# Scores of two batches in one set of 64x64 tiles, and routing per pair of batches, in an attention and soft-MoE kernel

## The chip, the cores and the metric

One core of one Trainium2 chip runs the kernel. Its engines are PE (TensorE: matmuls into PSUM), DVE (VectorE), ACT (ScalarE), POOL (GpSimd) and SP (SyncE, which here issues every DMA). The metric is the device time of one launch in microseconds, and lower is better.

## The reference

Attention with pooled keys and values, and behind it a soft mixture of experts over all tokens:

```python
# q, k, v: (8 batches, 8 heads, 576 tokens, 64); phi: (8, 8, 576, 32)
a = softmax(phi, axis=2)                                   # over the 576 tokens
k_m = einsum('bhsm,bhsd->bhmd', a, k); v_m = einsum('bhsm,bhsd->bhmd', a, v)
attn = softmax(q @ k_m^T / 8, axis=-1)                     # over 32 pooled slots
x = (attn @ v_m) as (4608 tokens, 512)
logits = x @ moe_phi                                       # (4608, 32)
d = softmax(logits, axis=0)                                # over all 4608 tokens
slot_input = d.T @ x                                       # (32, 512): 4 slots for each of 8 experts
slot_out[e] = relu(slot_input[e] @ w1[e]) @ w2[e]          # 512 -> 1024 -> 512
out = softmax(logits, axis=1) @ slot_out                   # (4608, 512)
```

All data is fp32. The inputs q, k, v and phi are 33 MB, the weights 33.6 MB, the output 9.4 MB.

## The kernel before

`x` is never formed. Per batch, `pool_phi` and `pool_kv` make the pooled keys and values; the pooled values times `moe_phi` (`mphd`) then turn attention probabilities straight into logits.

The code does not issue its instructions in the order in which it is written. Each step is handed to a planner (`Plan.add`) with an engine, an assumed cost, the tiles it reads and writes, and a priority. `Plan.order` goes through the steps as a list scheduler does: of those that could start first by the assumed costs it takes the one with the smallest priority, and it hands out buffers (`Slots`) as they come free. What results is a fixed order for each engine. Without a priority of its own a step has its number in the code, plus `plan.bias`: 60 less for the pooling (so it comes ahead), 110 more for the routing (behind).

One batch goes like this. `pool_phi` takes the maximum of phi over tokens (L498 on DVE, L506 to L531), subtracts it on POOL (L536), takes the exponential on ACT (L542) and sums over tokens (L549 on POOL, L559 on PE, L566 and L567 on DVE). `pool_kv` multiplies phi with k and v on PE (L586), scales on ACT (L602, L609), turns the pooled keys and values by PE (L620, L621) and multiplies the values with `moe_phi` (L629). `attend` turns q in 32x32 blocks on DVE (`q_blocks`, L665), and then goes through two halves `a` of a batch: `scores` on PE (L698: 16 matmuls on 32x32 tiles of the array into `scbank`), a DVE transpose that reads `scbank` (L712), the softmax (maximum L729 on DVE, subtraction L734 on POOL, exponential L739 on ACT, sum L744 on DVE, L749 on ACT, reciprocal L753 on DVE, product L757 on POOL), a DVE transpose of the probabilities (L762), and `transposed`: PE transposes (L773) with ACT copies (L778), which put tokens on partitions and heads and slots on columns. `logits` multiplies the probabilities with the value products (L793), copies (L805), turns by PE (L811) and copies (L818) into `L`, 96 partitions of tokens.

`route` is the token softmax of one batch: the maximum over its tokens (L831, L838, L843, L849), the difference (L857), the exponential (L866), the routing sums of probabilities (L875, the 96 tokens of a group as contraction), and from them the batch's share of `slot_input` (L897, L901, L908, L925), stored in `SIU` with its maximum in `MB` and its sum in `SD`. The merge (L960 to L991) scales the eight batches to a common maximum and adds them up into `SIM`, on DVE for the most part. Then come the experts on PE (L1055, L1080, L1104), with the token-side softmax (`slots`, L1128 to L1167) beside them, and the output (L1194 to L1226, stores L1234).

Space: most buffers lie in one SBUF tile, `arena`, of 44,288 columns. Attention's buffers are stacked from its start, 30,172 columns; the weights come in 19 slots of 2,048 columns (1 MB) that fill it from its end. So six slots are free from the start, and the others as attention gives up its buffers. The 32 weight loads stand in SP's one queue with the inputs; 13 of them go into a slot for the second time, after an expert has read the first load. Filler matmuls (L463) stand on PE where the planner finds it idle, at the start and at the end of attention.

Of the kernel before, what the change touches and what calls it, by code (L numbers as in the profile page):

```python
# [20 lines left out]
class Plan:  # L21
# [14 lines left out]
    def __init__(self):  # L36
        self.ops = []
        self.last_w = {}
        self.reads = {}
        self.bias = 0  # L40

    def add(self, eng, cost, fn, r=(), w=(), also=(), pri=None, dma=0.0, slack=0.0):
        i = len(self.ops)
        deps = set()
        tiles = set()
        for x in r:
            for key in x:
                tiles.add(key[0])
                if key in self.last_w:
                    deps.add(self.last_w[key])  # L50
        for x in w:
            for key in x:
                tiles.add(key[0])
# [15 lines left out]
        self.ops.append((eng, cost, fn, deps, i + self.bias if pri is None else pri, dma, tiles, need, slack))  # L69
# [177 lines left out]
def kernel(  # L247
# [38 lines left out]
    JG = 3  # L286
    NG = J // JG
    Y = 32
    R = HALF // Y
    T = JG * Y  # L290
    X = R * NG
    U = R * J
    JY = J * Y

# [17 lines left out]
    b_o = Slots(banks, [(i, 1) for i in range(4)], (b_m,))  # L312
# [5 lines left out]
    PHI_SZ, KV_SZ, AT_SZ = C * J * M, 2 * C * J * D, X * (2 * CM + 2)  # L318
    Q_SZ, QT_SZ, KT_SZ, EX_SZ, TR_SZ = C * J * D, C * J * D // 2, 3 * P, 2 * U * M, 2 * U * Y
# [10 lines left out]
    def shaped(off, shape):  # L330
# [4 lines left out]
        if len(shape) == 2:  # L335
            a = a.rearrange("p (a b) -> p a b", a=shape[0])
        elif len(shape) == 3:
            a = a.rearrange("p (a b c) -> p a b c", a=shape[0], b=shape[1])
# [8 lines left out]
    def stack(shape, n, fifo=False):  # L347
# [11 lines left out]
    NSEG = B  # L359
    mphi_b = stack([C, NS], 1).tile()  # L360
    kps = stack([2, P], 2)
    dm1s, wdgs = stack([NS], 2), stack([NS], 2)
    vms = stack([2, D], 4, fifo=True)
    vprs = stack([2, NS], 3, fifo=True)
    lgTs = stack([R, T], 2)
    trees = stack([C, 4, M], 1)
    pmxs, pmbs, pess = stack([C, M], 2), stack([C, M], 2), stack([C, M], 2)
    dfs = stack([X, NS], 2)
    wts = stack([2 * CM + 2], 2)
    wtbs = stack([2, C, NS], 2)  # L370
# [6 lines left out]
    attns = stack([AT_SZ], 2, fifo=True)  # L377
    aTs, sexs = stack([TR_SZ], 2), stack([EX_SZ], 2)
    kTs, qTs = stack([KT_SZ], 2, fifo=True), stack([QT_SZ], 3)
# [12 lines left out]
    repa_b = keep("repa", [P, NS])  # L392
    ones_b = keep("ones", [P, P])
    mphd_b = keep("mphd", [P, C, 2, NS])
    ident, maskhp, maskc, rep, repa, ones, mphd = (
        x.ap for x in (ident_b, maskhp_b, maskc_b, rep_b, repa_b, ones_b, mphd_b)
# [6 lines left out]
    P_AHEAD, R_BEHIND = 60, 110  # L403
# [3 lines left out]
    def f():  # L407
        nc.vector.memset(ones, 1.0)
        for i in range(2):
            a = attns.aps[i].rearrange("p (x y) -> p x y", x=X)  # L410
            nc.vector.memset(a[:, :, 2 * CM:], 1.0)
# [859 lines left out]
```

## Time and profile before

Three runs of the kernel: 229.35, 230.9 (the median) and 231.32 us. The profiled execution has a span of 229.8 us; the page gives no other time of it.

| What | Profiled execution |
|---|---|
| first DVE transpose of scores (L712) | 24.9 us |
| last q turned (L665) | from 120.0 us |
| merge begins (L960) | 146.8 us |
| first expert matmul (L1055) | 155.3 us |
| first matmul with the last weights (L1104) | 195.6 us |
| end | 229.8 us |
| busy: PE, DVE, ACT, POOL | 185.0, 139.3, 86.9, 85.0 us |
| moved by DMA | 76.5 MB, 333 GB/s over the span |

Times count from the first instruction. Engines wait for each other by semaphores; the profile names for each idle stretch of an engine the instruction that ended it. A matmul's own duration overlaps with those of its neighbours, so for PE the busy time of a group is read, not the mean of one. L numbers are lines of the kernel, as in the listing above.

### The profile page before, as it was taken

What the parts mean: (1) busy time and instruction counts of PE and PEld (TensorE: products, weight loads), DVE (VectorE), ACT (ScalarE), POOL (GpSimd) and SP (SyncE); (2) the same over time, 40 slices, a digit from 0 to 9 for tenths busy, and PEclk for the clock granted to TensorE, in tenths of its full rate; (3) what the DMA queues carried; (4) which work ended last, traced back from release to release, by engine and by line L of the source; (5) the groups of instructions that cost most, each with busy time, mean ns of one, the idle gap of its engine ahead of it and who ended that gap; (6) DMA issues with size and microseconds to landing.
All of it is one profiled execution on the core that took longest, in us unless ns stands there. A gap on an engine that the chain in (4) does not pass through costs nothing.

```text
span 229.8 us, 6394 instructions
## 1 busy us (share of the span) xinstructions
PE 185.0 (81%) x2772; PEld 109.7 (48%) x2772; DVE 139.3 (61%) x241; ACT 86.9 (38%) x230; POOL 85.0 (37%) x83
## 2 busy tenths in 40 slices
PE   8998939959978988899887979939999985599400
PEld 6786615626646636644644556624553421164100
DVE  3244696978499887856786681699401960277410
ACT  2022332562654754635546655300102332176300
POOL 2370773998159479266495432030000000000000
PEclk9999995995997997755999988985999999769655
DMA  6999999999999999994592999657999997059994
GB/s 225 383 380 389 379 389 378 393 399 383 347 393 395 387 387 401 345 392 152 185 369 63 418 356 396 240 184 277 347 415 409 409 409 298 0 205 409 414 414 203
DMA packets 27884, 76.50 MB, mean 333 GB/s; under 512 B 1744, under 2 KB 5840, under 8 KB 27856
## 3 DMA queue, kind: packets, MB, share of 16 engines
q1 hardware_dynamic: 27856, 76.09, 87.8%
q8 instruction: 22, 0.36, 0.6%
q14 instruction: 6, 0.05, 0.1%
HBM read 66.65 MB, written 9.44 MB: 331 GB/s over the span
## 4 chain that ended last, share of the span: by engine, by line
PE 44%; DMA 25%; DVE 13%; SPq 4%; ACT 3%; issue 3%; POOL 2%; DVEq 0%; ACTq 0%; POOLq 0%
DMA top<-in_q_dram 13%; DMA arena<-in_moe_w_dram 8%; PE kvbank L586 7%; PE bank L1055 7%; PE scbank L698 5%; PE bank L773 5%; SPq L445 4%; DMA out_dram<-arena 4%; PE bank L1215 3%; PE bank L875 3%; PE bank L793 3%; PE kvbank L1104 2%; PE kvbank L463 2%; DVE arena L665 2%; POOL arena L536 1%
## 5 line engine op out<-in xcount | busy, mean ns | idle before, releaser
L536 POOL TENSOR_TENSOR arena<-arena 128x1152 f32<-128x1152 f32 x8 | 21.0, 2631 | 26.8 <-ACT arena L531 26.8
L463 PE MATMUL kvbank<-ones 128*128 128x256 f32 x90 | 26.9, 441 | 2.1 <-ACT arena L609 1.1
L665 DVE STREAM_TRANSPOSE arena<-top 128x1152 f32<-128x1152 f32 x16 | 21.7, 1360 | 9.1 <-DMA top<-in_q_dram 9.1
L698 PE MATMUL scbank<-arena 32*32 32x288 f32 x512 | 23.1, 471 | 2.8 <-DVE arena L712 2.8
L586 PE MATMUL kvbank<-arena 64*32 64x128 f32 x1152 | 24.0, 315 | 1.2 <-issue 0.9
L549 POOL TENSOR_TENSOR arena<-arena 128x128 f32<-128x128 f32 (+2 forms) x32 | 23.3, 729 | 4.3 <-ACT arena L542 2.4
L757 POOL TENSOR_TENSOR arena<-arena,ssm 128x576 f32<-128x576 f32 x16 | 18.5, 1156 | 16.4 <-DVE ssm L753 16.4
L586 PEld LDWEIGHTS kvbank<-arena 64*32 64x32 f32 x1152 | 19.7, 122 | 7.0 <-issue 3.4
L463 PEld LDWEIGHTS kvbank<-ones 128*128 128x128 f32 x90 | 18.3, 218 | 6.6 <-issue 1.8
L734 POOL TENSOR_TENSOR arena<-arena,smx 128x576 f32<-128x576 f32 x16 | 18.5, 1158 | 7.8 <-DVE smx L729 7.8
L778 ACT COPY arena<-bank 96x384 f32<-96x384 f32 x32 | 14.4, 475 | 17.5 <-PE bank L773 17.3
L712 DVE STREAM_TRANSPOSE arena<-scbank 128x576 f32<-128x576 f32 x16 | 12.3, 768 | 12.5 <-PE scbank L698 12.5
L773 PE MATMUL bank<-ident,arena 128*96 128x128 f32 x96 | 18.1, 339 | 1.5 <-DVE arena L762 1.2
L1055 PE MATMUL bank<-arena,SIM 128*32 128x256 f32 x256 | 16.6, 425 | 3.4 <-DVE SIM L991 3.4
L498 DVE TENSOR_REDUCE arena<-arena 128x128 f32<-128x1152 f32 x8 | 17.4, 2171 | 2.5 <-DMA arena<-in_phi_dram 2.5
L1104 PE MATMUL kvbank<-arena 128*32 128x512 f32 x128 | 15.6, 598 | 3.7 <-DMA arena<-in_moe_w_dram 3.7
L1215 PE MATMUL bank<-sr,cT 128*128 128x512 f32 x36 | 13.5, 508 | 5.0 <-ACT arena L1224 1.9
L773 PEld LDWEIGHTS bank<-ident,arena 128*96 128x96 f32 x96 | 13.2, 157 | 6.3 <-issue 2.7
L1226 DVE COPY arena<-bank 128x512 f32<-128x512 f32 x18 | 11.8, 690 | 6.7 <-DMA out_dram<-arena 3.7
L1055 PEld LDWEIGHTS bank<-arena,SIM 128*32 128x32 f32 x256 | 8.7, 123 | 10.8 <-DVE SIM L991 3.6
L698 PEld LDWEIGHTS scbank<-arena 32*32 32x32 f32 x512 | 8.6, 114 | 10.5 <-issue 4.2
L1224 ACT COPY arena<-bank 128x512 f32<-128x512 f32 x18 | 10.3, 587 | 8.2 <-DMA out_dram<-arena 4.0
(108 smaller groups left out, 264.5 us busy)
## 6 DMA issues: line engine op xcount, KB each, us to landing
arena<-in_moe_w_dram SPq DMA_DIRECT2D x32, 1024.0 KB, 10.6
arena<-in_k_dram SPq DMA_DIRECT2D x8, 1152.0 KB, 10.3
arena<-in_v_dram SPq DMA_DIRECT2D x8, 1152.0 KB, 12.1
top<-in_q_dram SPq DMA_DIRECT2D x8, 1152.0 KB, 14.0
out_dram<-arena SPq DMA_DIRECT2D x12, 768.0 KB, 9.4
arena<-in_phi_dram SPq DMA_DIRECT2D x8, 576.0 KB, 7.7
arena<-in_moe_phi_dram SPq DMA_DIRECT2D x1, 64.0 KB, 9.1
```

What stands on the lines that cost most here:

```text
L463: lambda: nc.tensor.matmul(warm.ap, ones, ones.unsqueeze(1).to_broadcast([P, 2, P]), start=True, stop=True,),
L536: lambda: nc.gpsimd.tensor_tensor(ph(), ph(), mb.ap.unsqueeze(2).to_broadcast([P, C, J, M]), op=ALU.subtract),
L549: plus = lambda o, x, y: nc.gpsimd.tensor_tensor(o, x, y, op=ALU.add)
L586: nc.tensor.matmul(acc.ap[M * c: M * c + M, a, : 2 * D], ph()[h0: h0 + HALF, c, j, :], kv()[h0: h0 + HALF, :, c, j * D: j * D + D], start= ...
L665: nc.vector.transpose(qT.ap.rearrange("p (i u y) -> p u i y", i=2, y=Y), qt.ap[:, h * QT_SZ: h * QT_SZ + QT_SZ].rearrange("p (u i x) -> p ...
L698: nc.tensor.matmul(scb.ap[M * c: M * c + M, r, :JY], kT.ap[h0: h0 + Y, i * P + M * c: i * P + M * c + M], qT[c // 2].ap.rearrange("p (i c ...
L734: lambda: nc.gpsimd.tensor_tensor(exv(), exv(), bc(mx), op=ALU.subtract),
L757: lambda: nc.gpsimd.tensor_tensor(exv(), exv(), bc(sm), op=ALU.mult),
L773: nc.tensor.transpose(tp.ap[:T, t * P: t * P + P], aT.ap[:, x: x + T], ident)
L1055: nc.tensor.matmul(hb.ap[NS * j: NS * j + NS, :256], SIM.ap[:, 2 * i + c, NS * e: NS * e + NS], wv[:, c, 256 * j: 256 * j + 256], start=(e ...
L1104: nc.tensor.matmul(pacc.ap[NS * x: NS * x + NS, 0, :DM], hT()[:, 4 * t + 2 * i + j, NS * e: NS * e + NS], wv[:, j, t, :], start=(e == 0 an ...
L1215: lambda po=po, i=i, ct=cT[bp, j0]: nc.tensor.matmul(po.ap[:, :DM], ct.ap()[:, i * P: i * P + P], sr.ap, start=True, stop=True),
```

## The change

A pair of batches takes the place of one batch. A batch's 576 tokens are 64 rows of 9 (`J`); the rows of two batches fill the 128 partitions.

- **Scores.** A round is now two heads (`c`) of both batches, four rounds per pair in place of two rounds per batch. The pooled keys are written block-diagonally (`kps`, with zeros set once; four PE transposes instead of two, into `kbs`), so that a 64x64 tile of the array takes both 32-row blocks of one head. A round is 8 matmuls, in place of 16 on 32x32 tiles. What DVE's transpose makes of them has tokens on partitions: batch `g`, token of 64; columns head, `J`, slot.
- **Transposes dropped.** Since the softmax already stands with tokens on partitions, `transposed` (L773, L778) goes. The routing sums read the softmax buffer `ex` itself, 288 columns at a time (a block of ones behind it gives the sums), in 18 matmuls per pair with 64 tokens as contraction.
- **Logits.** The value products are written block-diagonally into `vpb` (128x128 for each head). Eight matmuls on the whole array, two for each round, add up a pair's logits in one PSUM bank, which is set aside for them (`b_l`; the other small results have three banks instead of four). One DVE transpose (after's L955) brings them into `L`, 128 partitions of tokens, in place of two ACT copies and two PE transposes per batch.
- **Routing and merge.** `route` runs once per pair, on 128 partitions and 288 columns; the merge is over four segments. `slots` works on 128 partitions with 9 x 32 columns instead of 96 with 12 x 32.
- **Order.** The priorities are given by `plan.at(base, slope)`: pooling of pair `bp` from `bp - 1.15`, loads of q from `bp - 0.45`, score round `c` from `bp + 0.25 c`, routing from `bp + 1.2` (the last one from `bp + 1`). Some assumed costs are set anew, among them that of scores.
- **Loads and space.** The first loads are phi of batches 0 and 1, moe_phi, and then q, k, v of each. Attention's buffers take 34,436 columns of `arena`, so four of the 19 weight slots are free from the start.

The order on SP, at the start of the program. A row is one instruction (x and a count: so many alike in a row): its line, its name, what it writes and reads, the size; `top` holds q, `arena` all else. Before:

```order
L445 DMA arena<-in_phi_dram 128x4x288
L445 DMA arena<-in_k_dram 128x4x576
L445 DMA arena<-in_v_dram 128x4x576
L445 DMA arena<-in_moe_phi_dram 128x4x32
L445 DMA top<-in_q_dram 128x4x576
L445 DMA arena<-in_phi_dram 128x4x288
L445 DMA arena<-in_k_dram 128x4x576
L445 DMA arena<-in_v_dram 128x4x576
L445 DMA top<-in_q_dram 128x4x576
```

And now:

```order
L458 DMA arena<-in_phi_dram 128x4x288 x2
L458 DMA arena<-in_moe_phi_dram 128x4x32
L458 DMA top<-in_q_dram 128x4x576
L458 DMA arena<-in_k_dram 128x4x576
L458 DMA arena<-in_v_dram 128x4x576
L458 DMA top<-in_q_dram 128x4x576
L458 DMA arena<-in_k_dram 128x4x576
L458 DMA arena<-in_v_dram 128x4x576
```

The same nine loads come first; batch 1's v is the last of them now, batch 1's q was.

PE in the middle of attention. `bank` with a number is one of the four small PSUM banks (62 to 65; 65 is the one set aside now), `kvbank` the pooled sums, `scbank` the scores, `pmh` and `dmh` small maxima. Before (a round of scores is the first row, pooling of the next batch stands between):

```order
L698 MATMUL scbank<-arena 32x288 x16
L586 MATMUL kvbank<-arena 32x128 x24
L773 MATMUL bank_64<-ident,arena 96x128 x3
L773 MATMUL bank_62<-ident,arena 96x128 x3
L586 MATMUL kvbank<-arena 32x128 x24
L773 MATMUL bank_63<-ident,arena 96x128 x3
L773 MATMUL bank_65<-ident,arena 96x128 x3
L793 MATMUL bank_64<-arena 32x192 x6
L559 MATMUL bank_62<-maskhp,arena 128x2
L586 MATMUL kvbank<-arena 32x128 x24
L811 MATMUL bank_63<-ident,arena 96x96 x2
L875 MATMUL bank_65<-arena 32x258 x6
```

And now, with L599 for L586, L716 for L698, L785 for the logits and L810 for the maximum in `route`:

```order
L599 MATMUL kvbank<-arena 32x128 x48
L785 MATMUL bank_65<-arena 128x288 x2
L599 MATMUL kvbank<-arena 32x128 x24
L533 MATMUL bank_64<-ident,pmh_83 64x128 x2
L716 MATMUL scbank<-arena 64x288 x8
L572 MATMUL bank_62<-maskhp,arena 128x2
L810 MATMUL bank_63<-ident,arena 32x128
L716 MATMUL scbank<-arena 64x288 x8
L785 MATMUL bank_65<-arena 128x288 x2
L635 MATMUL bank_64<-ident,arena 128x4x32 x4
L640 MATMUL bank_62<-ident,arena 128x128
```

The transposes of probabilities are gone, and two logits matmuls follow each round of scores at some distance.

DVE at the end of attention, up to the first step of the merge. `ssm` and `smx` are sums and maxima of the softmax. Before:

```order
L744 TENSOR_REDUCE ssm_82<-arena 128x18
L762 STREAM_TRANSPOSE arena<-arena 128x576
L753 RECIPROCAL ssm_82<-ssm_82 128x18
L857 TENSOR_TENSOR arena<-L_93,bank_63 96x192
L762 STREAM_TRANSPOSE arena<-arena 128x576
L908 TENSOR_TENSOR arena<-bank_62,maskc 128x256
L831 TENSOR_REDUCE arena<-L_93 96x32
L843 TENSOR_REDUCE dmh_89<-bank_64 32x1
L857 TENSOR_TENSOR arena<-L_93,bank_62 96x192
L960 TENSOR_REDUCE m_95<-arena 128x32
```

And now:

```order
L890 TENSOR_TENSOR arena<-bank_64,maskc 128x512
L761 TENSOR_REDUCE ssm_81<-arena 128x18
L770 RECIPROCAL ssm_80<-ssm_80 128x18
L770 RECIPROCAL ssm_81<-ssm_81 128x18
L777 STREAM_TRANSPOSE arena<-arena 128x576 x2
L955 STREAM_TRANSPOSE L_92<-bank_65 128x288
L803 TENSOR_REDUCE arena<-L_92 128x32
L815 TENSOR_REDUCE dmh_88<-bank_62 32x1
L829 TENSOR_TENSOR arena<-L_92,bank_64 128x288
L969 TENSOR_REDUCE m_94<-arena 128x32
```

The last but one batch's mask product (L908) stood among the last rows; now that of the last but one pair (L890) is ahead of the last softmax sums, and one turn of logits stands where ACT copies fed DVE.

The diff, cut to its core:

```diff
 class Plan:
+    def at(self, base, slope=1.0):
+        self.phase = [base * 1000.0, slope]
...
+        if pri is None:
+            pri = self.phase[0]
+            self.phase[0] += self.phase[1]
...
-    b_m = Slots(banks, [(i, 1) for i in range(4)])
+    b_m = Slots(banks[:3], [(i, 1) for i in range(3)])
+    b_l = Slots(banks[3:], [(3, 1)])
...
-    FIRST = ["phi0", "k0", "v0", "mphi", "q0", "phi1", "k1", "v1", "q1"]
+    FIRST = ["phi0", "phi1", "mphi", "q0", "k0", "v0", "q1", "k1", "v1"]
...
+            for i in range(2):
+                for r in range(R):
+                    nc.tensor.transpose(o[:, i, :, r, :], kp.ap[:, i, r * P: r * P + P], ident)
...
+                    vpp.ap[HALF * g: HALF * g + HALF, HALF * c: HALF * c + HALF],
+                    vT.ap[:, c].rearrange("p r m -> p (r m)"),
+                    mphd[:, c].rearrange("p a n -> p (a n)"),
...
+                    tile_position=(0, HALF * g),
...
+            nc.scalar.copy(
+                vpb.ap[x: x + Y, :, x: x + NS],
+                vpp.ap[x: x + Y, : H * NS].rearrange("p (h n) -> p h n", h=H),
+            )
...
-    def scores(a, qT, kT, ex):
+    def scores(c, qT, kb, ex):
...
+                for a in range(2):
+                    for g in range(2):
+                        h0 = HALF * a
                         nc.tensor.matmul(
+                            scb.ap[HALF * g: HALF * g + HALF, a, :JY],
+                            kb[g].ap[h0: h0 + HALF, i, c].rearrange("p r m -> p (r m)"),
+                            qT[g][c // 2].ap.rearrange("p (i c x) -> p i c x", i=2, c=2)[
+                                h0: h0 + HALF, i, c % 2, :
                             ],
...
+                            tile_position=(h0, HALF * g),
...
-    def transposed(a, r, aT, atb):
-                nc.tensor.transpose(tp.ap[:T, t * P: t * P + P], aT.ap[:, x: x + T], ident)
...
+    def logits(c, aT, vpb, lp):
...
+                h = 2 * c + a
+                nc.tensor.matmul(
+                    lp.ap[:, :JY],
+                    vpb.ap[:, h, :],
+                    aT.ap[:, a * JY: (a + 1) * JY],
+                    start=(h == 0),
+                    stop=(h == H - 1),
                 )
...
-    def route(si, atb, vm):
+    def route(bp, ex, vm):
...
+            for j in range(J):
+                for g in range(2):
+                    x = NS * (j % 4)
                     nc.tensor.matmul(
+                        wp[g].ap[x: x + NS, : HM + M],
+                        dfv()[HALF * g: HALF * g + HALF, j, :],
+                        ev[HALF * g: HALF * g + HALF, :, j, :],
...
+                        tile_position=(HALF * g, x),
...
-    for b in range(B):
-        plan.bias = -P_AHEAD
...
+    for bp in range(NBP):
+        for g in range(2):
+            plan.at(bp - 1.15 + 0.5 * g, 8)
...
+        plan.at(bp - 0.45)
...
+        for c in range(C):
+            plan.at(bp + 0.25 * c, 15)
+            scores(c, qT, kb, ex)
+            aT = softmax(c, ex)
+            logits(c, aT, vpb, lp)
+        add(
+            DVE, dve(JN), lambda lp=lp, bp=bp: nc.vector.transpose(L[bp].ap, lp.ap[:, :JY]),
+            r=[lp], w=[L[bp]],
+        )
+        plan.at(bp + (1.2 if bp < NBP - 1 else 1.0), 10)
+        sip = route(bp, ex, vm)
```

More of the change, by code (lines that the diff above doesn't have):

```diff
@@ L44, in add @@
         deps = set()
-        tiles = set()
+        tiles = {}
         for x in r:
             for key in x:
-                tiles.add(key[0])
+                tiles[key[0]] = None
                 if key in self.last_w:
@@ L52, in add @@
             for key in x:
-                tiles.add(key[0])
+                tiles[key[0]] = None
                 if key in self.last_w:
@@ L391 @@
     rep_b = keep("rep", [P, 4, NS])
-    repa_b = keep("repa", [P, NS])
     ones_b = keep("ones", [P, P])
     mphd_b = keep("mphd", [P, C, 2, NS])
-    ident, maskhp, maskc, rep, repa, ones, mphd = (
-        x.ap for x in (ident_b, maskhp_b, maskc_b, rep_b, repa_b, ones_b, mphd_b)
+    ident, maskhp, maskc, rep, ones, mphd = (
+        x.ap for x in (ident_b, maskhp_b, maskc_b, rep_b, ones_b, mphd_b)
     )
@@ L668, in f @@
                 )
-            add(DVE, dve(QT_SZ), f, r=[qt], w=[qT])
-            halves.append(qT)
-        return halves
-    def attend(b, qt, kT, vp):
-        atb = attns.tile().split(2 * R)
-        Lb = L[b // 2]
-        qT = q_blocks(qt)
-        parts = [(0, 1), (1, 2)]
-        ex, aT = sexs.tile().split(2), aTs.tile().split(2)
-        for a0, a1 in parts:
-            for a in range(a0, a1):
-                scores(a, qT, kT, ex)
-            softmax(a0, a1, ex, aT)
-            for a in range(a0, a1):
-                for r in range(R):
-                    transposed(a, r, aT, atb)
-        logits(b, aT, vp, Lb)
-        return atb
-    def scores(a, qT, kT, ex):
+            halves.append((qT, f))
+        return halves
+    def scores(c, qT, kb, ex):
         scb = b_s2.tile()
@@ L893, in route @@
+        for g in range(2):
+            add(ACT, act(HM) + act(1), lambda f=f, g=g: f(g), r=[wp[g]], w=[wt.part(g)])
         wtp = b_m.tile()
         def f():
-            for a in range(2):
+            for g in range(2):
+                for a in range(2):
+                    x = NS * (2 * g + a)
+                    nc.tensor.matmul(
+                        wtp.ap[:, x: x + NS],
+                        wt.ap[:, g, P * a: P * a + P],
+                        rep[:, 0, :], start=True, stop=True,
+                    )
+            for g in range(2):
@@ L1151, in f @@
                 nc.vector.tensor_tensor(cr[:, :, r, 1, :], cx(), c4[:, :, r, 0, :], op=ALU.subtract)
-        add(DVE, 2.0, f, r=[cxb], w=[csb])
-        for t in range(NG):
+        add(DVE, 1.6, f, r=[cxb], w=[csb])
+        for t in range(J // G):
             tp, ct = b_m.tile(), cTs.tile()
```

430 lines of the change are left out of this document (200 added, 230 removed).

## The prediction

> **What bounds the kernel now.** I read the span first, then the busy time of the engines by stage, then the chain of waits, then the groups of instructions and who waited for whom.
>
> ```profile
> span 229.8 us, 6394 instructions
> 24.90:110.60 85.70, 73.58 (x1527) 45.45 (x1528) 68.47 (x104) 41.77 (x115) 56.62 (x53) 0.80 0.98 362
> 110.60:146.80 36.20, 31.74 (x480) 20.20 (x481) 23.06 (x48) 20.06 (x64) 15.81 (x14) 0.95 0.84 313
> 146.80:155.30 8.50, 4.46 (x32) 2.72 (x31) 7.78 (x13) 1.52 (x5) 2.02 (x1) 0.89 0.44 157
> ...
> 155.34 10.36 PE bank L1055 x144
> ...
> 176.34 19.19 DMA arena<-in_moe_w_dram
> 195.58 1.11 PE kvbank L1104 x8
> ```
>
> The three stage rows give the stretch in us and its length, then the busy us of PE, PE's weight loads, VectorE (DVE), ScalarE and GpSimd, each with its instruction count, then the granted TensorE clock, the DMA share and GB/s. The last three rows are pieces of the chain: start, length, what. Attention runs until 146.8, the merge until 155.3, where the first expert matmul (L1055) starts. From there to the end of the span lie 229.8 - 155.3 = 74.5 us. In them the kernel waits for weights: 13 of the 32 loads of 1 MB can only go into a slot that an expert has emptied, so the last 19 us before L1104 are DMA. That part moves with the start of the experts, one for one; I cost it at nothing, because the change leaves its loads, their number after the merge and their order as they are. So the question is when the first L1055 starts.
>
> In attention no engine is full: from 24.9 to 146.8 (121.9 us) PE is busy 73.58 + 31.74 = 105.3 us (86%), DVE 68.47 + 23.06 = 91.5 us (75%). DVE is idle for 30.4 us. Why, the waits say:
>
> ```profile
> DVE arena L712 <- PE scbank L698: 12.5, 9, 5.1
> DVE arena L665 <- DMA top<-in_q_dram: 9.1, 4, 6.5
> DVE prs L566 <- PE bank L559: 8.6, 5, 2.3
> DVE arena L908 <- PE bank L901: 4.0, 1, 4.0
> ...
> 24.89 0.78 DVE L712 STREAM_TRANSPOSE arena<-scbank 128x576 f32<-128x576 f32 x1 [5.05 <-PE scbank L698]
> ```
>
> The columns of the waits are total us, times and the longest. The first L712 (5.1) and the first L665 (6.5) lie before 24.9. After it DVE waits for PE 12.5 - 5.1 + 8.6 + 4.0 = 20.0 us of its 30.4, and for q 2.6 us. PE and DVE pass the work to and fro, and PE, whose instructions stand in one order, is mostly the later one.
>
> **The change part by part.** First PE, with what is dropped, the rows that price what is new, and the DVE groups:
>
> ```profile
> L773 PE MATMUL bank<-ident,arena 128*96 128x128 f32 x96 | 18.1, 339 | 1.5 <-DVE arena L762 1.2 <-DVE ssm L753 0.3
> L778 ACT COPY arena<-bank 96x384 f32<-96x384 f32 x32 | 14.4, 475 | 17.5 <-PE bank L773 17.3
> L875 PE MATMUL bank<-arena 96*32 96x258 f32 x96 | 10.0, 437 | 0.2 <-ACT arena L866 0.2
> L793 PE MATMUL bank<-arena 128*32 128x192 f32 x96 | 7.5, 356 | 0.0
> L811 PE MATMUL bank<-ident,arena 96*96 96x96 f32 x16 | 3.1, 275 | 0.8 <-issue 0.8
> L629 PE MATMUL bank<-mphd,arena 128*32 128x64 f32 x64 | 2.8, 252 | 0.6 <-ACT arena L624 0.6
> L620 PE MATMUL bank<-ident,arena 128*128 128x128 f32 x16 | 3.4, 297 | 3.0 <-ACT arena L602 2.9 <-ACT arena L918 0.2
> L897 PE MATMUL bank<-repa,arena 96*128 96x32 f32 x32 | 4.8, 273 | 0.0
> L698 PE MATMUL scbank<-arena 32*32 32x288 f32 x512 | 23.1, 471 | 2.8 <-DVE arena L712 2.8
> L831 DVE TENSOR_REDUCE arena<-L 96x32 f32<-96x192 f32 x8 | 3.7, 459 | 1.7 <-ACT L L818 1.7
> L857 DVE TENSOR_TENSOR arena<-L,bank 96x192 f32<-96x192 f32 x8 | 2.7, 338 | 0.7 <-PE bank L849 0.7
> L908 DVE TENSOR_TENSOR arena<-bank,maskc 128x256 f32<-128x256 f32 x8 | 3.3, 417 | 4.2 <-PE bank L901 4.0
> L712 DVE STREAM_TRANSPOSE arena<-scbank 128x576 f32<-128x576 f32 x16 | 12.3, 768 | 12.5 <-PE scbank L698 12.5
> L498 DVE TENSOR_REDUCE arena<-arena 128x128 f32<-128x1152 f32 x8 | 17.4, 2171 | 2.5 <-DMA arena<-in_phi_dram 2.5
> L665 DVE STREAM_TRANSPOSE arena<-top 128x1152 f32<-128x1152 f32 x16 | 21.7, 1360 | 9.1 <-DMA top<-in_q_dram 9.1
> ...
> 136.66 2.08 PE L463 MATMUL kvbank<-ones 128*128 128x256 f32 x4
> ...
> 146.09 1.56 PE L463 MATMUL kvbank<-ones 128*128 128x256 f32 x6
> ```
>
> Busy us stand after the bar, then mean ns of one; since matmuls overlap, I price by busy us per record, and an fp32 matmul leaves two records. Gone from PE: the transposes of probabilities L773 (18.1), the old logits L793 and their turn L811 (7.5 + 3.1), the old token sums L875 (10.0), the old value products L629 (2.8): 41.5 us. New on PE:
>
> - Logits: 8 matmuls per pair of batches on the whole array, 288 columns, so 64 records. A full 128x128 record of 256 columns takes 1.56/6 = 0.26 us where the clock is full (146.09) and 2.08/4 = 0.52 us at its slowest (136.66); times 288/256 that is 0.29 or 0.585 us. I take the fast one, 18.7 us; the slow end is 37.4.
> - Token sums: 144 records. With eight tiles of the array at work instead of three, L875's time scales by records, columns and tiles to 10.0 x (144 x 288 x 3)/(96 x 258 x 8) = 6.3 us; if the tiles don't overlap better than now, 10.0 x 144/96 = 15.0. I take 6.3, since L698 with eight tiles does 512 records in 23.1 us.
> - Value products: 64 records on one tile position, from 2.8 (as now) to 9.6 (64 at L897's 4.8/32 = 0.15): I take 5.
> - Transposes of the pooled keys: 16 more at L620's 3.4/16 = 0.21: 3.4 us.
> - Scores: half as many records on tiles four times as large, four at a time instead of eight: the same array time, so 0.
>
> That is 33.4 us taken (bounds 31 and 65), so PE loses 41.5 - 33.4 = 8 us of 105 (bounds: 10 less, 24 more). ScalarE loses L778's 14.4 us and gains copies; it was busy 61.8 of 121.9 us, so neither counts.
>
> DVE's softmax groups keep their counts and shapes. Four reduces, subtractions and mask products replace eight, on 288, 288 and 512 columns instead of 192, 192 and 256: by size 4 x 0.459 x 1.5 = 2.8 for 3.7, 4 x 0.338 x 1.5 = 2.0 for 2.7, and 4 x 0.417 x 2 = 3.3 for 3.3. Four new transposes of logits at half of L712's 0.768 add 1.5. Sum 0 (bounds 1 each way).
>
> The start. The scores of a pair need the pooled keys of both its batches, so the first ones wait for the second batch's v.
>
> ```profile
> 26.91 2.25 PE L586 MATMUL kvbank<-arena 64*32 64x128 f32 x144
> ...
> 19.48 0.62 ACT L602 ACTIVATE arena<-kvbank,prs 128x128 f32<-128x128 f32 x2 [6.44 <-PE kvbank L463]
> ...
> 26.63 1.38 DVE arena L665
> ```
>
> The first nine loads are the same bytes in both kernels; the last of them, q of batch 1, lands at 26.6 (L665 starts). Now v of batch 1 is last, so the pooling (2.25 us) ends near 29. From ScalarE's pooled keys (19.48) to the first score transpose (24.89) the old kernel took 5.4 us, with filler matmuls between; with a little less of that I put the first score transpose at 33.5, which is 8.6 us later. DVE does not lose all of it: three L498 and four L665 (3 x 2.17 + 4 x 1.36 = 12) stand ahead of it in place of two each (7), and the two row maxima and reciprocals behind them add about 1: 6 us of later work is done by then. Net +2.7 (bounds 0 and 5).
>
> DVE's idle time. Two thirds of it (20.0 of 30.4) is waiting for PE. Where PE is asked for 8 us less, at least 8 x 20.0/30.4 = 5.3 us of that should go; the 4.0 us that DVE waited in the last stretch for L901 are behind other softmax work in the new order, so I take 7 (bounds 0 and 20).
>
> The merge, 8.5 us now, works on four segments instead of eight:
>
> ```profile
> 148.34 1.09 DVE L969 TENSOR_TENSOR arena<-arena 128x896 f32<-128x896 f32 x1 [0.48 <-ACT arena L966]
> 149.46 1.68 DVE L972 TENSOR_REDUCE arena<-arena 128x128 f32<-128x896 f32 x1
> ```
>
> Three stored segments instead of seven: 2.77 x 4/7 = 1.6 us less (bounds 0, if the last token sums come later than DVE, and 2.5).
>
> Loads. Four weight loads instead of six fit before attention gives up its space; two more (2 x 1 MB at 313 GB/s = 6.7 us) must pass between the last inputs and the experts. DMA stood idle 16% of 36.2 and 56% of 8.5 us there, 10.6 us: they fit, and the inputs end earlier by as much. Zero, with 3 as the other end.
>
> Sum: +2.7 - 7 - 1.6 = -5.9 us, all ahead of the first L1055: it starts at 149.4, and the span is 223.9. The three runs have a median of 230.9, 1.1 above the profiled span; the page shows no time around that execution's span, so I add the same 1.1: **225.0 us**.
>
> **The rivals.** A change below 1% (2.3 us) can't be told from none here.
>
> *PE was the whole brake.* If DVE's waiting for PE all goes (20.0), the next limit is the input.
>
> ```profile
> 119.97 1.37 DVE L665 STREAM_TRANSPOSE arena<-top 128x1152 f32<-128x1152 f32 x1
> ```
>
> The inputs and four weight loads, 37.3 MB at the stretch's 362 GB/s, are in at 103; from the last L665 to the experts the old kernel needed 155.3 - 120 = 35 us. So 138, 17 us earlier: 214 us. For it: PE's 86%. Against: the last pair turns its q and runs four softmax rounds after that point, not two.
>
> *No change.* The idle time keeps its length, with waits for PE replaced by those of a larger unit: a pair's logits close only when its fourth round is done, and one PSUM bank holds them. Then +2.7 - 1.6 = +1.1, 232 us. For it: the first scores come 8.6 of a pair's 121.9/4 = 30 us later, and DVE can't be refilled from another pair.
>
> *Slower: the clock.* If gaps in PE's work bring its clock down, the new matmuls cost more than the transposes that they replace.
>
> ```profile
> 44.00:50.00 6.00, 3.47 (x137) 2.40 (x121) 5.43 (x11) 2.47 (x9) 5.77 (x6) 1.00 1.04 406
> 50.00:56.00 6.00, 5.80 (x119) 3.66 (x127) 4.83 (x8) 2.96 (x8) 5.76 (x8) 0.58 1.05 378
> 98.00:104.00 6.00, 6.00 (x69) 2.88 (x75) 3.71 (x4) 2.34 (x7) 3.78 (x2) 0.50 1.05 392
> 110.00:116.00 6.00, 4.99 (x107) 3.31 (x88) 4.08 (x10) 3.56 (x13) 2.99 (x2) 1.00 0.71 255
> ```
>
> After a stretch in which PE was busy 3.47 of 6 us the clock was 0.58. If PE, with less to do, stays there, the logits cost 37.4 us and the sums and products up to 15.0 and 9.6: 24 us more on PE in all, and by the same two thirds 16 us on the path; in full that is +17 (248 us), half way 240. It decides from 2 us more on PE than now (0.66 x 3.5 + 1.1 = 2.3 above zero), that is, from a granted clock between 25 and 110 well under the 0.80 of now. Against it: at 98 to 104 the clock was 0.50 with PE busy all 6 us, and at 110 to 116 it was 1.00 with 4.99, so gaps alone don't set it. The Trainium skill ("TensorE: Matmul & The Clock Gate", Part 1) says that an idle window of about 3.4 us halves the clock and that activity releases it: by that rule less PE work is a risk, and the first two rows agree, the last two don't. The same page (Part 4) says that transposes don't count as activity: by it, dropping 96 of them raises the clock, which speaks against this rival.
>
> That the transposes are not dropped is excluded: they don't stand in the new order.
>
> **How the numbers follow.** Forecast 0.50, its own range 219 to 229. PE the whole brake 0.16 (214). No change 0.18 (229 to 233). The clock 0.16 (236 to 248). Faster by over 1% is the forecast but for its last tenth, and the first rival: 0.62; within 1%: 0.04 + 0.18 = 0.22; slower: 0.16. For 8 in 10 the range runs from 213, just past the first rival, to 236, where the clock's case begins; it leaves out about 0.04 below and 0.14 above.
>
> **What would show it.** Right: the first score transpose near 33, the first expert matmul near 149 and the same 74 us behind it; DVE's waits for PE between them near 13 us; logits near 19 us of PE, token sums near 6. The merge below 7 us. Wrong: a first L1055 after 153 with DVE's idle time still at 30 (no change), PE's total between 25 and the experts above 105 with a clock under 0.7 (the clock), or a tail longer than 75 us because weights come later (the loads, which I set to zero).

## The result, and the profile after

The changed kernel takes 223.3 us (median of four runs, 221.8 to 226.8) where the kernel before takes 230.8: a ratio of 0.967, with a 95% interval of 0.960 to 0.975. Run again later it was 0.967 (0.961 to 0.973). Ratios, here and below, leave out runs more than 1.5% above the fastest of the same kernel; medians and ranges are of all runs. The profiled execution's own time was 221.8, its span 220.1. Its first line of the page, then its four stages (attention from the first score transpose to the merge, the merge, the experts to the last weights, the output), and behind them the row of before that answers to the first:

```profile
span 220.1 us, 5624 instructions
```

```profile
32.83:138.75 105.92, 88.08 (x1491) 57.11 (x1491) 84.06 (x133) 42.67 (x119) 68.54 (x62) 0.95 0.93 347
138.75:147.65 8.90, 3.83 (x56) 2.70 (x56) 6.19 (x13) 1.59 (x7) 2.02 (x1) 0.87 0.99 373
147.65:187.44 39.79, 35.76 (x416) 15.92 (x416) 16.25 (x42) 7.50 (x18) 0.00 (x0) 0.94 0.97 380
187.44:220.10 32.66, 16.03 (x46) 7.81 (x46) 13.18 (x20) 10.79 (x19) 0.00 (x0) 0.69 0.71 289
```

```profile
24.89:146.80 121.91, 105.33 (x2006) 65.67 (x2007) 91.53 (x152) 61.83 (x179) 72.44 (x67) 0.85 0.94 347
```

Columns as in the prediction: stretch, length, busy us of PE, its weight loads, DVE, ScalarE and GpSimd, the granted clock, DMA share, GB/s. Attention begins 7.9 us later and ends 8.05 earlier, so it is 16.0 us shorter (105.9 for 121.9). PE's busy time in it falls by 17.2 us, at a granted clock of 0.95 where it was 0.85. The merge is not shorter (8.9 for 8.5 us). The experts take 0.5 us less, the output 1.5 less, at 289 GB/s for 276.

The groups of the new kernel, and who waited for whom:

```profile
L716 PE MATMUL scbank<-arena 64*64 64x288 f32 x256 | 21.6, 433 | 3.0 <-DVE arena L730 2.5 <-DVE prs L579 0.5
L785 PE MATMUL bank<-arena 128*128 128x288 f32 x64 | 21.4, 464 | 2.6 <-DVE arena L777 2.6
L599 PE MATMUL kvbank<-arena 64*32 64x128 f32 x1152 | 20.2, 273 | 2.2 <-issue 1.5 <-ACT arena L555 0.7
L849 PE MATMUL bank<-arena 64*32 64x288 f32 x144 | 7.5, 408 | 1.2 <-DVE m L969 1.2
L635 PE MATMUL bank<-ident,arena 128*128 128x128 f32 x32 | 5.9, 317 | 1.4 <-ACT arena L615 1.4
L662 PE MATMUL bank<-mphd,arena 128*64 128x64 f32 x64 | 5.7, 235 | 0.0
```

```profile
L586 PE MATMUL kvbank<-arena 64*32 64x128 f32 x1152 | 24.0, 315 | 1.2 <-issue 0.9 <-ACT arena L542 0.2
```

```profile
DVE arena L730 <- PE scbank L716: 8.9, 7, 3.1
DVE L L955 <- PE bank L785: 4.9, 3, 2.7
DVE arena L777 <- POOL arena L774: 3.7, 3, 2.5
```

A piece of DVE's timeline in the new merge (start, length, what, and the idle time before it with what ended it), and the group of before that answers to its slowest operation, L990:

```profile
142.86 0.69 DVE L890 TENSOR_TENSOR arena<-bank,maskc 128x512 f32<-128x512 f32 x1 [1.84 <-PE bank L881]
...
144.53 1.90 DVE L990 TENSOR_SCALAR st<-st 128x32 f32<-128x32 f32 x1
```

```profile
L981 DVE TENSOR_SCALAR st<-st 128x32 f32<-128x32 f32 x1 | 1.6, 1633 | 0.0
```

Logits (L785), sums (L849) and value products (L662) are each within 3 us of their prices. The row that the forecast did not expect to move is L599 (new), which is L586 of before: the pooling, the same 1152 records of the same shape, takes 20.2 us where it took 24.0. The granted clock is what differs. That made the clock the question for the runs.

### The profile page after: what moved, and what is told of

It is laid out like the page before. It is cut to its first block, busy times and chain, and to the rows that moved or that the text cites. A ratio compares the mean times of both kernels' runs of the same rounds, so it can differ in the third digit from the quotient of the medians.

```text
span 220.1 us, 5624 instructions
## 1 busy us (share of the span) xinstructions
PE 172.5 (78%) x2418; PEld 105.3 (48%) x2418; DVE 135.5 (62%) x230; ACT 71.4 (32%) x182; POOL 86.7 (39%) x85
## 3 DMA queue, kind: packets, MB, share of 16 engines
q1 hardware_dynamic: 27856, 76.09, 91.1%
## 4 chain that ended last, share of the span: by engine, by line
PE 41%; DMA 22%; DVE 14%; POOL 9%; issue 5%; ACT 2%; SPq 1%; DVEq 0%; POOLq 0%
DMA top<-in_q_dram 10%; DMA arena<-in_moe_w_dram 9%; PE bank L1064 7%; PE kvbank L476 6%; PE bank L785 5%; PE scbank L716 4%; PE bank L1220 4%; PE kvbank L599 3%; DMA out_dram<-arena 3%; DVE arena L700 3%; POOL arena L774 3%; POOL arena L562 3%; PE bank L849 2%; PE kvbank L1113 2%; POOL arena L751 2%
## 5 line engine op out<-in xcount | busy, mean ns | idle before, releaser
L476 PE MATMUL kvbank<-ones 128*128 128x256 f32 x92 | 25.4, 419 | 2.2 <-ACT arena L622 1.1
L716 PE MATMUL scbank<-arena 64*64 64x288 f32 x256 | 21.6, 433 | 3.0 <-DVE arena L730 2.5
L785 PE MATMUL bank<-arena 128*128 128x288 f32 x64 | 21.4, 464 | 2.6 <-DVE arena L777 2.6
L751 POOL TENSOR_TENSOR arena<-arena,smx 128x576 f32<-128x576 f32 x16 | 18.4, 1158 | 11.5 <-DVE smx L746 11.5
L599 PE MATMUL kvbank<-arena 64*32 64x128 f32 x1152 | 20.2, 273 | 2.2 <-issue 1.5
L476 PEld LDWEIGHTS kvbank<-ones 128*128 128x128 f32 x92 | 18.1, 207 | 6.7 <-issue 1.6
L599 PEld LDWEIGHTS kvbank<-arena 64*32 64x32 f32 x1152 | 16.2, 106 | 6.3 <-issue 3.9
L785 PEld LDWEIGHTS bank<-arena 128*128 128x128 f32 x64 | 12.1, 206 | 8.1 <-DVE arena L777 3.8
L777 DVE STREAM_TRANSPOSE arena<-arena 128x576 f32<-128x576 f32 x16 | 12.1, 758 | 3.8 <-POOL arena L774 3.7
L716 PEld LDWEIGHTS scbank<-arena 64*64 64x64 f32 x256 | 9.0, 137 | 10.8 <-DVE arena L730 4.5
L756 ACT ACTIVATE arena<-arena 128x576 f32<-128x576 f32 x16 | 11.0, 688 | 8.4 <-POOL arena L751 8.4
L1064 PEld LDWEIGHTS bank<-arena,SIM 128*32 128x32 f32 x256 | 8.6, 121 | 10.7 <-DVE SIM L1000 3.6
```

Source lines behind the costliest of these rows:

```text
L476: lambda: nc.tensor.matmul(warm.ap, ones, ones.unsqueeze(1).to_broadcast([P, 2, P]), start=True, stop=True,),
L599: nc.tensor.matmul(acc.ap[M * c: M * c + M, a, : 2 * D], ph()[h0: h0 + HALF, c, j, :], kv()[h0: h0 + HALF, :, c, j * D: j * D + D], start= ...
L716: nc.tensor.matmul(scb.ap[HALF * g: HALF * g + HALF, a, :JY], kb[g].ap[h0: h0 + HALF, i, c].rearrange("p r m -> p (r m)"), qT[g][c // 2].a ...
L751: lambda: nc.gpsimd.tensor_tensor(exv(), exv(), bc(mx), op=ALU.subtract),
L785: nc.tensor.matmul(lp.ap[:, :JY], vpb.ap[:, h, :], aT.ap[:, a * JY: (a + 1) * JY], start=(h == 0), stop=(h == H - 1),)
L1064: nc.tensor.matmul(hb.ap[NS * j: NS * j + NS, :256], SIM.ap[:, 2 * i + c, NS * e: NS * e + NS], wv[:, c, 256 * j: 256 * j + 256], start=(e ...
```

## The experiments

Theory 1 is the prediction's: PE is asked for less, and two thirds of that comes off the path. Theory 2 gives the gain to the new order, theory 3 to a clock that transposes don't hold up; theory 4 came out of the first four runs. Each run's row is the stage row from its first score transpose to its merge.

**Less work for PE in the old kernel.**

```diff
-            nc.vector.memset(a[:, :, 2 * CM:], 1.0)
+            nc.vector.memset(a, 1.0)
...
-                nc.tensor.transpose(tp.ap[:T, t * P: t * P + P], aT.ap[:, x: x + T], ident)
+            pass
...
-            lambda: nc.scalar.copy(
...
+            lambda: None,
```

> The kernel before, with the 96 transposes of probabilities on PE (18.1 us) and their 32 copies on ScalarE (14.4 us) left out and nothing else changed: the order of every other instruction is that of before. Routing then works on constants in place of the probabilities. Theory 1 (what the new kernel wins, it wins because PE is asked for less, and two thirds of that comes off the path): 18.1 x 0.66 = 12 us less, near 219; DVE's waits for PE fall from 20 us to under 12. Theory 2 (the gain is the new order and the shared tiles, not PE's relief): 228 to 231. Theory 3 (transposes don't keep the clock up): the granted clock between 25 and 110 us rises from 0.80 to over 0.90.

Measured: 227.1 us (220.9 to 232.0; before, beside it, 231.0).

```profile
25.18:147.11 121.93, 105.85 (x1910) 59.34 (x1911) 91.36 (x152) 48.16 (x147) 72.50 (x67) 0.71 0.93 344
```

In the profiled execution (229.3) 18 us of PE's work are gone and PE is busy as long as before, 105.9 us, because the clock fell from 0.85 to 0.71. Theory 3's rise of the clock did not come: over the whole span it was 0.785 to 0.845 in the four runs, 0.826 to 0.861 in those of the kernel before beside them. Theory 1 is not decided by this: the fastest of the four, 220.9, is near its 219, the others are not. The trace's clock changes only every 3.41 us; five such windows of this kernel, one a row, show that it isn't idle time that halves it:

```profile
93.84:97.25 3.41, 2.95 (x44) 1.19 (x44) 2.42 (x6) 0.79 (x3) 2.65 (x2) 0.50 1.05 377
97.25:100.66 3.41, 3.41 (x53) 1.41 (x45) 3.04 (x4) 1.41 (x4) 2.30 (x2) 0.50 1.06 385
100.66:104.08 3.42, 3.42 (x54) 1.35 (x46) 2.95 (x4) 1.70 (x5) 2.69 (x4) 0.50 1.05 391
104.08:107.49 3.41, 3.41 (x136) 3.09 (x120) 1.54 (x3) 0.42 (x2) 2.45 (x3) 0.50 0.53 195
107.49:110.91 3.42, 2.43 (x28) 1.78 (x20) 2.23 (x7) 2.47 (x10) 0.25 (x1) 1.00 0.56 175
```

PE is busy all through the second and third window, with scores on 32x32 tiles and small tiles of routing, and the next window is again at half; after the fourth, full of pooling on 64x32 tiles, eight at a time, it is full.

**The transposes put back into the new kernel, and the old kernel planned with a truer cost.**

```diff
+            for t in range(6):
+                z = tb.ap[:96, P * (t % 4): P * (t % 4) + P]
+                nc.tensor.transpose(z, aT.ap[:, 96 * t: 96 * t + 96], ident)
```

> The changed kernel, with 96 transposes of probabilities put back on PE (six of 96 columns ahead of each round's logits, into a bank that nobody reads); the order of everything else on DVE, ScalarE, GpSimd and SyncE is unchanged. Theory 1: PE is asked for 18 us more, two thirds of it comes back on the path: 223.3 + 12 = 235, so slower than the kernel before. Theory 2: little, 223 to 226. Theory 3: the granted clock between 33 and 110 us falls from 0.96 to about 0.80.

Measured: 233.4 us, ratio to before 1.013 (1.003 to 1.023).

```profile
32.69:147.62 114.93, 98.67 (x1587) 67.40 (x1587) 84.44 (x133) 42.50 (x119) 68.66 (x62) 0.94 0.88 321
```

PE is busy 10.6 us longer and attention is 9.0 us longer; the clock stays at 0.94. Theory 1's 235 is nearly met; theory 2's 223 to 226 is not, and theory 3 falls for good.

```diff
-        add(PE, pe(4 * R * C, M, JY, tiles=8), f, r=[*qT, kT], w=[scb], also=[ex])
+        add(PE, 1.2, f, r=[*qT, kT], w=[scb], also=[ex])
```

> The kernel before, with one number of the planner changed: scores are entered at 1.2 us per half (they are entered at 0.53 before; the trace has 23.1 us / 16 = 1.44). Only the order of instructions changes. Theory 1: 230.8 give or take 2. Theory 2 (the changed kernel gains by planning with truer costs): half of the gain or more, 223 to 227.

Measured: 236.3 us, ratio 1.018 (1.004 to 1.031). The row is of the slowest of its four runs, 241.7:

```profile
25.14:155.83 130.69, 114.75 (x2012) 70.64 (x2013) 91.17 (x151) 62.27 (x179) 72.52 (x67) 0.78 0.88 325
```

Truer costs made it slower: the other order comes with a clock of 0.78, and PE's time and attention both grow by some 9 us. This part of theory 2 falls; no run gives the old kernel the whole new order.

**Theory 4: the array's work sets the clock.** For each matmul record I took rows x columns of the array used x columns streamed, and summed them over every 3.41 us window between 20 and 185 us of all fourteen traces of this study, as a share of what the full array does at full clock: sixteen records of 128x128x256 in a window, 0.213 us each (the fillers' records start 0.216 us apart where the clock is 1.00). A window's clock is full where the window before it did at least 0.335 of that, half where it did less: this holds for 663 of 678 windows, in the kernel with the most windows at half (without the transposes) for 47 of 48. The threshold was fitted to the same windows. For comparison, 539 of the 678 are at full clock; the best threshold on PE's busy time holds for 589, and with transposes counted as nothing it is 625. The five windows above have shares of 0.22, 0.26, 0.26, 0.49 and 0.29. Over attention the share is 0.39 before and 0.55 after. The next two runs changed that share on purpose.

```diff
-                    vpb.ap[:, h, :],
-                    aT.ap[:, a * JY: (a + 1) * JY],
+                    vpb.ap[:Y, h, :],
+                    aT.ap[:Y, a * JY: (a + 1) * JY],
```

> The changed kernel with its 32 logits matmuls fed from 32 of the array's 128 rows: the same instructions, columns streamed and order, a quarter of the array's work, wrong logits. Theory 1 and the theory that idle time sets the clock: no change, 223.3, clock 0.96 between 33 and 110. Theory 4: the mean work between 33 and 138 us falls from 0.55 to 0.44 of full, 7 instead of 4 of its 31 windows lie under a third, and a window at half clock does less in turn: the granted clock between 33 and 138 falls from 0.96 to 0.80 to 0.90, the time rises by 3 us or more.

Measured: 232.9 us (230.1 to 235.6); its ratio to before is 1.000 (0.994 to 1.005). The row is of a run at 235.6:

```profile
32.76:152.19 119.43, 106.94 (x1491) 66.39 (x1491) 84.39 (x134) 42.57 (x119) 68.51 (x62) 0.79 0.84 309
```

The same 1491 records in the same order, PE's time up by 18.9 us, the whole gain gone. The share of array work is 0.39, that of the kernel before. The other groups show that it is the clock:

```profile
L716 PE MATMUL scbank<-arena 64*64 64x288 f32 x256 | 25.5, 503 | 2.7 <-DVE arena L730 2.2 <-DVE prs L579 0.5
L599 PE MATMUL kvbank<-arena 64*32 64x128 f32 x1152 | 24.7, 318 | 1.3 <-issue 1.3
```

Neither was touched; they took 21.6 and 20.2.

```diff
-                x = a * U * M + (r * NG + t) * T
-                nc.tensor.transpose(tp.ap[:T, t * P: t * P + P], aT.ap[:, x: x + T], ident)
+                x = min(a * U * M + (r * NG + t) * T, (a + 1) * U * M - P)
+                nc.tensor.matmul(
+                    tp.ap[:, t * P: t * P + P], ident, aT.ap[:, x: x + P], start=True, stop=True
+                )
```

> The kernel before, with each of its 96 transposes of probabilities (out 96x128) replaced by a matmul of the identity with 128 columns of the same data (out 128x128), so its routing works on wrong numbers; order, banks, copies and waits are those of before. PE is asked for more: a full matmul of 128 columns takes 0.26 us at full clock against 0.19 for a transpose, 7 us in all. Theory 1 (PE's work counts): 7 x 0.66 = 4.6 us slower, 235. Theory 4, formed from the runs so far (the clock of a window of 3.41 us is full when the array did at least a third of its full work in the window before: rows x columns used x columns streamed; idle time as such doesn't count, transposes do): the mean work between 25 and 147 us rises from 0.39 to 0.49 of full, the granted clock there from 0.85 to 0.92 or more, and the extra work costs nothing: 226 to 230.

Measured: 235.8 us, ratio 1.022 (1.017 to 1.027).

```profile
25.10:151.29 126.19, 109.91 (x2102) 76.39 (x2103) 91.87 (x152) 62.52 (x179) 72.39 (x67) 0.91 0.91 336
```

Its group of the replaced instructions:

```profile
L773 PE MATMUL bank<-arena,ident 128*128 128x128 f32 x192 | 28.6, 302 | 2.6 <-issue 1.5 <-DVE arena L762 0.8 <-DVE ssm L753 0.3
```

Here the clock did what theory 4 says (0.85 to 0.91, share 0.48) and the time did not. L773 grew by 10.5 us (18.1 to 28.6), not by 7; everything else on PE got 5.9 us faster; the net is 4.6 on PE and 4.3 on attention. Work added for the clock's sake is paid back in part only.

**DVE, the first loads, the merge.**

```diff
-                mx.ap, ph().rearrange("p c j m -> p c m j"), axis=AX.X, op=ALU.max
+                mx.ap, ph().rearrange("p c j m -> p c m j")[:, :, :, :1], axis=AX.X, op=ALU.max
```

> The changed kernel with DVE's maximum of phi taken over one of the nine tokens that it covers (L511, 17 us in all, to about 3; values stay near the reference's, since it is only the offset of the exponent). DVE is asked for 14 us less, PE for the same. If the time of PE (work by clock) is the brake of attention: 0 to 4 us less, 220 to 224. If DVE is the brake as much as PE: 8 us less or more, 215 or below.

Measured: 223.0 us, ratio to before 0.962 (0.955 to 0.969). Beside it ran the changed kernel:

> The changed kernel once more, beside the three others of this call on one chip: 223 to 225.

Measured: 223.7 us, ratio 0.967 (0.961 to 0.973), so the two can't be told apart. The row of the run with less for DVE:

```profile
32.94:137.63 104.69, 87.98 (x1491) 57.36 (x1490) 75.85 (x133) 42.55 (x119) 68.44 (x62) 0.95 0.95 351
```

DVE does 8.2 us less in attention, PE the same, and attention is 1.2 us shorter. DVE is not the brake.

```diff
-    FIRST = ["phi0", "phi1", "mphi", "q0", "k0", "v0", "q1", "k1", "v1"]
+    FIRST = ["phi0", "k0", "v0", "mphi", "q0", "phi1", "k1", "v1", "q1"]
```

> The changed kernel with the first nine loads in the order of before (all of batch 0, then all of batch 1). It tests the term of the start: the first score transpose came at 32.8 because the last v, of batch 1, lands last. In this order q of batch 1 lands last, v before it: the first scores could come 1 to 2 us earlier, but the second batch's q is needed for them as well. As predicted (the start costs 2.7 because the first pair needs all nine loads): within 1 us of 223.3. If the order of the first loads were the price: 221 or less, or, if the new order was worth something, 225 or more.

Measured: 230.7 us, ratio to before 0.997 (0.993 to 1.001), 7 us more than the changed kernel. The planner had made another order from it: the first score transpose came at 35.68, 2.9 us later, and the rest was lost behind it.

```profile
35.68:145.10 109.42, 89.88 (x1491) 59.47 (x1491) 84.72 (x134) 42.22 (x119) 66.92 (x61) 0.92 0.89 327
```

So the same nine loads were permuted with every engine's order held:

```diff
+        nine = [i for i in seq if self.ops[i][0] == SP][:9]
+        seq = [i for i in seq if i not in nine]
+        for i in [nine[m] for m in (0, 4, 5, 2, 3, 1, 7, 8, 6)] + seq:
```

> The changed kernel with only its first nine loads issued in the order of before (batch 0, then batch 1); every engine's order stays that of the changed kernel. In e4_first the planner was given the old order of loads as well, and put its own order after it: 230.7. If the loads themselves cost that: 228 or more here. If it was the order that the planner then made: the last of the nine loads lands when it did, q in place of v, and the first score transpose comes at 32.8 give or take 1: 222 to 225.

Measured: 235.2 us, ratio to before 1.015 (1.008 to 1.022): 11.5 us more. Neither expectation had this. PE and DVE in its trace:

```profile
18.21 0.48 PE L522 MATMUL bank<-ident,arena 128*128 128x128 f32 x1 [8.85 <-DVE arena L514]
```

```profile
16.07 2.08 DVE L514 TENSOR_REDUCE arena<-arena 128x128 f32<-128x1152 f32 x1 [8.88 <-DMA arena<-in_phi_dram]
43.92 0.78 DVE L733 STREAM_TRANSPOSE arena<-scbank 128x576 f32<-128x576 f32 x1 [2.71 <-PE scbank L719]
```

```profile
43.92:150.89 106.97, 90.46 (x1491) 58.71 (x1491) 84.34 (x134) 42.65 (x119) 68.51 (x62) 0.92 0.90 333
```

Phi of the second batch lands at 16 us, and PE's order has its transpose second: PE stands still for 8.9 us behind it, with the pooling of batch 0, whose inputs were there, queued. The first scores come 11.1 us later, attention keeps its length (107.0 for 105.9), and the time rises by as much. While PE stood still none of its later work was done, and a delay of that kind at the start is paid in full at the end.

```diff
-    add(POOL, 2.0, lambda: nc.gpsimd.memset(hTb.ap, 0.0), r=[SIM], w=[hTb])
...
+        nc.gpsimd.tensor_copy(hTb.ap[:, :1], SIM.ap[:, 0, :1])
+        nc.gpsimd.memset(hTb.ap, 0.0)
...
+    add(POOL, 2.0, f, r=[SIM], w=[hTb])
```

> The changed kernel, with GpSimd's zeroing of the hidden layer (2.0 us, 144.4 to 146.4 in the trace) made to wait for the merge's last result. If the merge missed its term because a 128x32 operation of DVE (L990) stood for 1.9 us beside that zeroing: L990 falls to about 0.3 us, the merge from 8.9 to about 7.2, the time by 1.6 to about 221.7. If L990 is slow by itself: no change, 223.3.

Measured: 223.7 us, ratio to before 0.971 (0.960 to 0.982): no change against the changed kernel. L990 in DVE's timeline, and two pieces of the chain:

```profile
145.48 0.18 DVE L990 TENSOR_SCALAR st<-st 128x32 f32<-128x32 f32 x1
```

```profile
146.90 9.49 PE bank L1069 x144
188.29 1.98 PE kvbank L1118 x8
```

The cause of the slow operation is shown: 1.90 us beside GpSimd's zeroing (2.02 us from 144.38), 0.18 without it, and this merge (from 139.71) took 7.2 us. The gain did not reach the end: the last weights came 48.6 us after the merge began, in the new kernel 48.7 (138.75 to 187.44). DMA is at 0.99 in the merge of the new kernel (0.44 before), so the weights, not the merge, set the time from there; that reading is from the rows, not from a run that takes loads away.

**Fillers at the tail.**

```diff
+                for _ in range(3 if e >= E - 3 else 0):
+                    nc.tensor.matmul(
+                        scbank[:, 0, :256], ones, ones.unsqueeze(1).to_broadcast([P, 2, P]),
+                        start=True, stop=True,
+                    )
```

> The changed kernel with three full matmuls (128x128x256, into a bank that nobody reads) ahead of each of the last six groups of expert matmuls, where PE waits 1.4 us for each load of weights. Theory 4: in the changed kernel the clock is half from 189.7 to 196.5, after three windows with little work; with the fillers it stays full there, the last expert matmuls, the sum over experts (128x512) and the first output products take half as long, 1 to 2 us less: 221.5 to 222.5. If the clock follows something else, or the output is bound by its transfers anyway: 223.3 or a little more.

Measured: 227.1 us, ratio to before 0.983 (0.978 to 0.989), worse than the changed kernel.

```profile
190.62 1.56 PE L1109 MATMUL scbank<-ones 128*128 128x256 f32 x6
192.11 1.06 PE L1118 MATMUL kvbank<-arena 128*32 128x512 f32 x8
194.09 1.10 PE L1204 MATMUL bank<-arena,rep 128*128 128x512 f32 x2 [0.91 <-DVE arena L1199]
```

The clock held and the sum over experts (L1204) took 1.10 us, but the last expert matmul came at 192.1 in place of 187.4. Three fillers take about 1.5 us, and in the changed kernel PE waits that long (1.48 and 1.40 us) ahead of the last two groups only; ahead of the first of the six it doesn't wait, so there the fillers push the experts back. With one filler in each of the last four groups, and the late zeroing (the edit is against the run with three):

```diff
-                for _ in range(3 if e >= E - 3 else 0):
+                if e >= E - 2:
```

> The changed kernel with GpSimd's zeroing moved behind the merge (as in e5_late_zero) and one full matmul, not three, ahead of each of the last four groups of expert matmuls: 0.52 us where PE waits 1.4 us for weights. In e8_tail_fill three took 1.56 us and put the last expert matmul 4.6 us late, but the clock stayed full and the sum over experts took 1.10 us in place of 1.75. If the array's work sets the clock: full from 187 to 194, the last matmul on time, 0.7 to 1 us less than the changed kernel. If one full matmul is too little to hold it: the same as the changed kernel.

Measured: 223.2 us; 223.7 for the changed kernel beside it, with intervals that overlap (0.950 to 0.965 and 0.961 to 0.973 of before). The clock was full from 187 to 195 (0.67 and 0.89 there in two executions of the changed kernel), but in its profiled execution (224.0) the last expert matmul came at 190.9, not on time, against 187.4 and 188.4 in those two. Whether the full clock is worth half a microsecond stays open.

## Why the prediction was right, and where it was wrong

The time was right (225.0 against 223.3), and so was the engine: PE is what DVE waits for. The reason was not: PE is asked for no less than before, it runs at a higher clock. That its relief came out at the forecast size is luck. The rows ahead of the first score transpose, before and now:

```profile
0.00:24.89 24.89, 22.55 (x262) 17.14 (x263) 8.99 (x16) 4.70 (x10) 10.49 (x16) 1.00 0.97 347
0.00:32.83 32.83, 28.76 (x411) 21.77 (x412) 15.79 (x24) 8.83 (x20) 16.11 (x23) 1.00 0.99 359
```

- **The sum in its own terms.** It goes by DVE's time, and up to the merge all its terms were near. The first score transpose was put at 33.5 and came at 32.8. DVE had done 6.8 us of later work by then (15.79 less 8.99; 6 forecast), so +1.1 for +2.7. Its idle time in attention fell from 30.4 to 21.9 us, -8.5 for -7; its work to the merge fell by 0.7, for 0. Together 8.0 earlier, where 4.3 was forecast. DVE's waits for PE were 6.8 (8.9 less the first, 2.1) + 4.9 = 11.7 us, where 13 was forecast.
- **The step that failed: "PE loses 8 us".** What is dropped was priced as the old kernel ran it, partly at half clock (41.5 us), the logits at full clock. Busy time times granted clock, up to the first expert matmul, is 22.55 x 1.00 + 105.33 x 0.85 + 4.46 x 0.89 = 116.0 us before and 28.76 x 1.00 + 88.08 x 0.95 + 3.83 x 0.87 = 115.8 now. With the clock taken record by record and the fillers left out it is 91.1 and 92.5: the five dropped groups come to 33.6 us at full clock, the logits, sums and value products to 32.0, the scores, the pooling and the keys' transposes grew by 3.8 together and the other groups fell by about 1. So PE is asked for nothing less. It is busy 11.7 us less by then (132.3 to 120.7) because the clock rose, and that term was set to zero. The thin logits undid the rise and cost all of the gain: 88.08 x 0.95/0.79 gives 105.9 us for their clock, and 106.9 was measured.
- **The start, by PE's time.** PE's 17.2 us less in attention are not all clock. Fillers left out, PE does 5.9 us of work ahead of the first score transpose before and 10.9 now; 288 of the 1152 pooling records stand there in place of 144. I estimate those 5.0 us at 5.0/0.85 = 5.9 at the old clock of attention, so the start costs about 7.9 - 5.9 = +2.0, the clock gives -11.3, and with +1.3 for the rest that is the 8.0. That DVE's own later work pays for the start, as the forecast had it, is not borne out: 8 us less work for DVE were worth 0.7. The permuted loads moved the start by 11.1 with no more of PE's work done by then (10.7 us at full clock, fillers left out, for 10.9), and the time by 11.5.
- **DVE's idle time, "two thirds".** Attention's length less PE's busy time is 16.6 us before and 17.8 after. It is 16.1 without the transposes, 16.3 with them put back, 15.9 with truer costs, 16.3 with dense matmuls, 16.5 with permuted loads and 16.7 with less for DVE; only the thin logits (12.5) and the old loads planned anew (19.5) stand apart. So PE's time counts nearly in full in most of these runs (9.0 of 10.6 us with the transposes put back, 4.3 of 4.6 with dense matmuls), and by 0.72 with the thin logits (13.5 of 18.9).
- **The merge, -1.6.** Measured +0.4. The operations on segments did shrink, by 1.6 us; what was missed is DVE's wait of 1.84 us behind the last token sums (the bound of zero named it), and L990. Of the latter the Trainium skill ("SBUF — State Buffer", "Who interferes with whom") says that a tensor_scalar can need the ports that DVE shares with GpSimd and then blocks until GpSimd's instruction ends; the two rows of the late zeroing agree (1.90 and 0.18 us). It was 1.63 us in the kernel before too, beside the same zeroing, so it explains little of the difference.
- **"Moves one for one".** From the first expert to the end it was 72.4 us, not 74.5; most of that is the output's rate. With the late zeroing it stopped being so: DMA has no slack left after attention.
- **The rivals.** "PE the whole brake" needed all of DVE's waits for PE to go (20.0 us); 11.7 are left, since PE is asked for no less. "No change" would have been right for the same instructions with the array's work of before. The clock's rival moved the right quantity the wrong way: the condition was gaps in PE's work, and it is the array's work that counts. The Trainium skill ("TensorE: Matmul & The Clock Gate", Part 1), cited there, has the window right, 3.41 us in the trace; idle time doesn't decide here, since PE busy for 3.41 of 3.41 us kept half the clock. Part 4 of the same page of the Trainium skill, that transposes don't count, is not borne out: without the transposes the clock fell to 0.71, with them put back it stayed at 0.94.

## What to carry to other kernels

PE's time is its work divided by its clock, and the clock is bought with array work: before replacing wide matmuls by small ones, or dropping "useless" ones, price what goes and what comes at the same clock, and count rows x columns x columns streamed per 3.4 us against a third of the full array. A zero-padded matmul on the whole array can be cheaper than one on fewer rows, because everything beside it runs at full clock (223.7 us against 232.9 with the thin logits); fillers that lengthen PE's queue were not. And a forecast that comes out right should still be taken apart: here the terms in DVE's time held, and the 8 us that PE was to be relieved of were a rise of its clock.

## What the runs showed of the hardware

The granted clock is half or full for windows of 3.41 us, and follows the array work of the window before (663 of 678 windows, threshold a third of the full array). A transpose's record counts like a matmul's record of the same shape (it leaves one, an fp32 matmul two). A kernel near the threshold, like the one before (0.39 on the mean), keeps switching: leaving out 18 us of PE's work gave runs from 220.9 to 232.0 us. A 128x32 tensor_scalar on DVE waited out a GpSimd memset of 2.02 us, ten times its own 0.18 us.
